# Unpadded value rows, and due times and port flags for the dense layer's first f64 splits

## The chip, the cores and the metric

The kernel runs on one core of one Trainium2 chip. The metric is the time of one execution on the device in microseconds; of several executions the median is taken. A profiled execution is one more run, with the hardware profiler on.

## What is computed

Three layers follow each other on 3072 tokens of 384 numbers (4 batches of 768 positions; 8 heads of 48):

```python
state = alpha[:, :, t, :, None] * state + einsum('bhd,bhe->bhde', k[:, :, t], v[:, :, t])
y[:, :, t] = einsum('bhd,bhde->bhe', q[:, :, t], state)          # for each position t

noisy = x @ w_gate + log1p(exp(x @ w_noise)) * noise             # 8 experts, the best two of each token
out[mask] += top2_w[mask, k, None] * (maximum(x[mask] @ w1[e], 0) @ w2[e])   # w1 384 x 1024

h = x @ w_in                                                     # 384 x 2048, float64 weights
return (maximum(0.01 * h, h) @ w_out).astype(float32)
```

The first is attention with a decaying state, the second a mixture of experts, the third a dense layer. Its two weight matrices are float64, all other inputs are float32.

## The kernel before

**Stages.** Attention takes 24 chunks of 128 positions (`build_unit(u)`). A chunk has three loads on SP's queue: decays `at` (L1058), keys and queries `kq` (L1062), values `nv` (L1066), with 5, 4 and 5 buffers. VectorE scans the decays (L1083, L1090) and scales keys and queries (L1104, L1110); TensorE makes the scores (L1145), the state's update (L1180, with 48 columns of a head's values) and the chunk's output (L1205, with 64 columns of a head's values as the stationary block, so that the two heads of a pair fill partitions 0 to 63 and 64 to 127). Values come padded from 48 to 64 columns for each head, so the columns above 48 are zero. The output is turned by a matmul with `turn_w` (L1235), whose rows 48 to 63 and 112 to 127 are zero, so what stands in those rows of the output has no effect. Every four chunks the tokens are routed: VectorE ranks the experts, and GpSimd scatters the rows (L1341) to `x_s`.

The experts then run as 16 groups of rows (two for each of 8 experts; expert 7's are groups 14 and 15), and the dense layer as 7 groups of tokens (16 to 22). A group has 8 steps (experts) or 16 steps (dense) of a first product (L808, nine matmuls into `ph`), an activation on ScalarE and VectorE (`hh`, `hl`), and a second product (L856, into `py`), which follows two steps later (LAG = 2). Each float32 factor is split into a high and a low part, and three products are added. A group of the dense layer first fetches the two expert results of each of its tokens by row (L888, GpSimd), weighs and adds them (`combine`, L895 on ScalarE and L897 on VectorE), and turns them (L622).

**Weights.** A pair is the weights of two steps. Expert weights are fetched and split into high and low parts by ScalarE (L523) and by VectorE or GpSimd (L527). The dense layer's float64 weights are the pairs E * NP to E * NP + 7 (`last_weights`): each is fetched in five parts, and each part goes through a chain of seven steps (`f64_split`): ScalarE scales (L344, L345), VectorE shifts (L349), joins (L352) and masks (L356), ScalarE rounds (L360), VectorE subtracts (L364), GpSimd multiplies and adds (L367, L368). Both results are stored in `w_d` (L552) and loaded again when a slot for weights is free (L557). Buffers for two chains exist (F64B = 2).

**The order of the work.** Nothing is scheduled by hand: while the program is built, a planner takes all steps (`Planner.add`), each with an engine, a duration, what it waits for, and a due time, and simulates the engines. `prepare` works due times back from a step's users (minus their durations, 0.8 us where the engine changes) and through the buffer rings; after that it takes the lower of this and the step's `own`. `run` picks for an engine the step that can start first, and among those the one that is due first; that order becomes the order of the engine's queue. A step with `port=True` on VectorE or GpSimd also starts, in the plan, no earlier than the last such step on either of the two ended. Loads with a `size` (in MB) pass one after another through a planned DMA of 0.25 MB/us. The plan adds no wait on the chip; the chip waits for data and buffers alone. A step that ran with `port` before: masks, decay and carry of attention, the low parts of expert weights (L527), routing's last part.

## Time and profile before

| | us |
|---|---|
| median of 3 runs | 1014.15 (1011.5 to 1016.0) |
| profiled execution | 1017.89 |
| its span, first to last instruction | 1016.2 |
| TensorE busy | 991.9 |
| VectorE busy | 554.9 |
| ScalarE busy | 378.1 |
| GpSimd busy | 253.8 |

Attention fills about the first 145 us of the span, the experts run to about 599 us and the dense layer to the end. A busy TensorE is not one at its peak: its matmuls overlap, so a matmul's own time says less than the distance from one start to the next. All times of rows below are microseconds from the span's start unless ns stands there. In the names of engines DVE is VectorE, ACT ScalarE, POOL GpSimd, PE TensorE, and SPq the queue of SyncE that issues loads and stores.

### The profile page before, as it was taken

The page shows a single profiled execution, that of the slowest core. Times are in us where ns is not written, and L with a number is a line of the kernel's source. Part 1 is how long each engine was busy: PE and PEld are TensorE (multiplying, and loading weights), DVE is VectorE, ACT ScalarE, POOL GpSimd, SP SyncE. Part 2 cuts the span into 40 slices and gives each one's busy share as a digit, 9 for nine tenths or more (in the row PEclk, how much of TensorE's full clock was granted, in tenths as well). Part 3 has the DMA queues.
Part 4 walks back from the last instruction along what each step waited for, and adds up shares of the span by engine and source line. Part 5 has one row for each costly group of instructions (what it writes and reads, how often), then busy time and mean ns, then how long its engine had stood idle before and what let it go on. Part 6 is the DMA issues. An engine that isn't in the chain of part 4 may idle for free.

```text
span 1016.2 us, 17660 instructions
## 1 busy us (share of the span) xinstructions
PE 991.9 (98%) x6533; PEld 940.4 (93%) x6533; DVE 554.9 (55%) x1208; ACT 378.1 (37%) x796; POOL 253.8 (25%) x311
## 2 busy tenths in 40 slices
PE   8999989999999999999999989999999999999997
PEld 7777879999999999999999989999999999999997
DVE  7998957224635546544644357645545445454543
ACT  5666555224534535454543233312212213121211
POOL 4376874002122314342212235301103002000000
PEclk9999999999999999999999999999999999999999
DMA  9988948423734546555568464301202102010000
GB/s 233 231 254 264 307 151 263 140 90 123 229 124 135 177 152 203 183 169 171 186 211 292 158 196 125 127 1 31 63 1 58 37 1 71 8 40 1 24 1 27
DMA packets 79091, 133.55 MB, mean 131 GB/s; under 512 B 8450, under 2 KB 56708, under 8 KB 78980
## 3 DMA queue, kind: packets, MB, share of 16 engines
q1 hardware_dynamic: 72852, 113.46, 36.4%
q0 software_dynamic: 6144, 18.88, 5.6%
q8 instruction: 53, 0.87, 0.4%
q14 instruction: 42, 0.34, 0.1%
HBM read 93.48 MB, written 39.62 MB: 131 GB/s over the span
## 4 chain that ended last, share of the span: by engine, by line
PE 85%; DMA 7%; DVE 4%; ACT 2%; issue 1%; POOL 1%; SPq 0%; ACTq 0%; DVEq 0%; POOLq 0%
PE ph L808 40%; PE py L856 39%; DMA at<-in_al_l_dram 4%; PE py L852 1%; PE pA L622 1%; PE pB L622 1%; DMA kq<-in_kq_l_dram 1%; DVE pT L1090 1%; PE pS L1145 1%; PE pY L1205 1%; DMA x_s<-xg,si 1%; DMA w2s<-in_moe_w_dram 1%; PE pA L1235 1%; DVE pF L1083 1%; DMA w1s<-in_moe_w_dram 1%
## 5 line engine op out<-in xcount | busy, mean ns | idle before, releaser
L856 PE MATMUL py<-w2hA,hh 128*128 128x384 f32 x768 | 220.6, 340 | 0.0
L856 PE MATMUL py<-w2hB,hh 128*128 128x384 f32 x768 | 217.2, 337 | 0.0
L836 DVE SCALAR_TENSOR_TENSOR hh<-ph,hh 128x384 fp32r<-128x384 f32 (+4 forms) x176 | 77.0, 460 | 178.9 <-ACT hh L826 178.4
L818 ACT ACTIVATE hc<-ph 128x384 f32<-128x384 f32 (+1 forms) x112 | 60.1, 537 | 295.2 <-PE ph L808 295.2
L821 DVE SCALAR_TENSOR_TENSOR hc<-hc 128x384 f32<-128x384 f32 (+1 forms) x112 | 69.5, 620 | 172.4 <-ACT hc L818 172.3
L826 ACT ACTIVATE hh<-ph 128x384 fp32r<-128x384 f32 (+4 forms) x128 | 65.0, 508 | 220.9 <-PE ph L808 184.0
L856 PEld LDWEIGHTS py<-w2hA,hh 128*128 128x128 f32 x768 | 141.0, 188 | 1.5
L856 PEld LDWEIGHTS py<-w2hB,hh 128*128 128x128 f32 x768 | 140.8, 188 | 1.5
L856 PE MATMUL py<-w2lA,hh 128*128 128x384 f32 x384 | 129.4, 337 | 0.0
L808 PE MATMUL ph<-xh,w1hB 128*128 128x384 f32 (+3 forms) x360 | 128.3, 356 | 0.8 <-ACT xh L626 0.6
L856 PE MATMUL py<-w2lB,hh 128*128 128x384 f32 x384 | 128.8, 335 | 0.0
L808 PE MATMUL ph<-xh,w1hA 128*128 128x384 f32 (+4 forms) x360 | 127.9, 355 | 0.1
L808 PE MATMUL ph<-xl,w1hB 128*128 128x384 f32 (+3 forms) x360 | 127.6, 354 | 0.0
L808 PE MATMUL ph<-xh,w1lB 128*128 128x384 f32 (+3 forms) x360 | 127.4, 354 | 0.0
L808 PE MATMUL ph<-xh,w1lA 128*128 128x384 f32 (+4 forms) x360 | 127.3, 353 | 0.0
L808 PE MATMUL ph<-xl,w1hA 128*128 128x384 f32 (+4 forms) x360 | 126.8, 352 | 0.0
L888 POOL DMA_INDIRECT xg<-y_d,gidx x48 | 49.7, 1036 | 255.7 <-PE pB L622 165.9
L856 PEld LDWEIGHTS py<-w2lA,hh 128*128 128x128 f32 x384 | 72.1, 188 | 1.4
L856 PEld LDWEIGHTS py<-w2lB,hh 128*128 128x128 f32 x384 | 72.1, 188 | 1.3
L808 PEld LDWEIGHTS ph<-xh,w1hB 128*128 128x128 f32 x360 | 68.1, 189 | 4.2 <-ACT xh L626 0.8
L808 PEld LDWEIGHTS ph<-xh,w1lA 128*128 128x128 f32 x360 | 67.6, 188 | 4.4
L808 PEld LDWEIGHTS ph<-xh,w1lB 128*128 128x128 f32 x360 | 68.0, 189 | 3.8
(187 smaller groups left out, 1513.0 us busy)
## 6 DMA issues: line engine op xcount, KB each, us to landing
w1s<-in_moe_w_dram SPq DMA_DIRECT2D x32, 384.0 KB, 4.2
w2s<-in_moe_w_dram SPq DMA_DIRECT2D x32, 384.0 KB, 4.4
kq<-in_kq_l_dram SPq DMA_DIRECT2D x24, 448.0 KB, 6.4
xg<-x_s SPq DMA_DIRECT2D x48, 192.0 KB, 2.5
y_d<-ys SPq DMA_DIRECT2D x48, 192.0 KB, 2.2
nv<-in_v_l_dram SPq DMA_DIRECT2D x24, 256.0 KB, 8.5
w1s<-in_moe_w_in_dram SPq DMA_DIRECT2D x24, 256.0 KB, 3.5
w2s<-in_moe_w_out_dram SPq DMA_DIRECT2D x16, 384.0 KB, 3.4
```

Of the source, the lines that this page charges most:

```text
L622: pe.last = nc.tensor.transpose(p[:, d, :n], src[:n, d * 128:(d + 1) * 128], identf[:n, :n])
L808: pe.last = nc.tensor.matmul(ps[:, :n], a[:, d, fo:fo + 128], x[:, d, :n], start=i == 0, stop=i == len(seq) - 1)
L818: nc.scalar.activation(hc[:, :n], ps[:, :n], AF.Copy)
L821: nc.vector.scalar_tensor_tensor(hc[:, :n], hc[:, :n], 0.01, hc[:, :n], op0=OP.mult, op1=OP.max)
L826: nc.scalar.activation(hh[:, :n], ps[:, :n], AF.Relu)
L836: nc.vector.scalar_tensor_tensor(dst, ps[:, a:b], 0.0, hh[:, a:b].bitcast(FT), op0=OP.max, op1=OP.subtract)
L852: pe.last = nc.tensor.matmul(py[:2 * n, :], HT[si, "both"][:, o:o + 2 * n], w[:, f % 2, :], start=(f == 0 and i == 0), stop=(f == nf - 1 a ...
L856: pe.last = nc.tensor.matmul(py[:n, :], h[:, o:o + n], w[:, f % 2, :], start=(f == 0 and i == 0), stop=(f == nf - 1 and i == 2))
L888: return nc.gpsimd.indirect_dma_start(out=yg, out_offset=None, in_=y_d[0:rows, :], in_offset=bass.IndirectOffsetOnAxis(ap=gidx[:, c, kk:kk ...
L1083: nc.vector.tensor_tensor_scan(rev(suf_f[:, 0:NW - 1]), rev(d["at"][:, 1:NW]), rev(heads_f[:, 1:NW]), 1.0, OP.mult, OP.add)
L1090: nc.vector.tensor_tensor_scan(wt, d["at"][:, i * half:(i + 1) * half], heads_f[:, i * half:(i + 1) * half], 0.0, OP.mult, OP.add)
L1145: pe.last = nc.tensor.matmul(d["pa", i][:, p], d["kt"][r, p], d["qp"][r, p], start=True, stop=True)
```

## The change

Values are stored for the kernel as rows of 8 x 48 numbers and 16 zeros (400 columns) in place of 8 x 64 (512). The buffer, the load's planned size (0.26 to 0.2 MB) and the two matmuls' slices follow. The stationary block of L1205 still has 64 columns; its last 16 are now the next head's first values.

In `last_weights` the seven steps of each chain of the first two dense pairs get an `own` due time, and in all eight pairs the steps 2, 5 and 6 of a chain (L352, L364, and L367 with L368) get `port`. The combine's second step (L897) gets `port` too.

```diff
@@ -769,10 +769,11 @@
                 k = 1.0 if m % 2 == 0 else 1.27
                 durs = (0.88, 0.43, 0.92, 0.58, 0.44, 0.46, 1.72)
                 chain = []
+                own = tm[0] + 15 + 10 * (i - E * NP) if i < E * NP + 2 else 1e9
                 for n, eng in enumerate("avvvavg"):
                     use = [(chain[0], r) for r in (R["f64"], R["f64o"])] if n else [(fe, R[nm])]
                     chain.append(add(eng, durs[n] * k, lambda m=m, n=n: split64(i, m, n), chain[-1:], use=use,
-                                     takes=[] if n else [R["f64"], R["f64o"]], phase=2))
+                                     takes=[] if n else [R["f64"], R["f64o"]], phase=2, own=own, port=n in (2, 5, 6)))
                 for which, st in enumerate((chain[4], chain[6])):
                     parts.append(add("s", 0.07, lambda m=m, which=which: spill64(i, m, which), [st],
                                      use=[(chain[0], R["f64o"])], size=0.13 * k, phase=2))
@@ -917,7 +918,7 @@
                     ga, gb = (add("g", 1.29, lambda j=j, kk=kk: gather2(key[2], j, kk), deps, takes=[R["xg"]], lat=3.0,
                                   phase=2, rows=2) for kk in range(2))
                     ca = add("a", 0.5, lambda j=j: combine(key[2], j, 0), use=[(ga, R["xg"])], phase=2)
-                    cb = add("v", 0.64, lambda j=j: combine(key[2], j, 1), [ca], use=[(ga, R["xg"]), (gb, R["xg"])], phase=2)
+                    cb = add("v", 0.64, lambda j=j: combine(key[2], j, 1), [ca], use=[(ga, R["xg"]), (gb, R["xg"])], phase=2, port=True)
                     GX[key + (j,)] = ga
                     AUX[key, j] = [cb]
                     ga.holders[R["xg"]].append(cb)
@@ -1062,12 +1063,12 @@
                 nc.sync.dma_start(d["kq"].rearrange("p a h c -> p (a h c)"), kq_l[u])
 
             def load_v():
-                d["v"] = loads.tile([128, H, 64], FT, name="nv", bufs=5)
-                nc.sync.dma_start(d["v"].rearrange("p h d -> p (h d)"), v_l[u * C:(u + 1) * C, :])
+                d["v"] = loads.tile([128, Dm + 64 - D], FT, name="nv", bufs=5)
+                nc.sync.dma_start(d["v"], v_l[u * C:(u + 1) * C, :])
 
             LA = d["LA"] = add("s", 0.46, load_al, takes=[R["at"]], size=0.23)
             LK = d["LK"] = add("s", 0.46, load_kq, takes=[R["kq"]], size=0.46)
-            LV = d["LV"] = add("s", 0.46, load_v, takes=[R["nv"]], size=0.26)
+            LV = d["LV"] = add("s", 0.46, load_v, takes=[R["nv"]], size=0.2)
 
             def check():
 
@@ -1177,7 +1178,7 @@
                     for p in range(HP):
                         for i in range(2):
                             r = slice(64 * i, min(64 * i + 64, PP))
-                            pe.last = nc.tensor.matmul(d["pu"][r, p, :], d["kN"][:, p, r], d["v"][:, 2 * p + i, 0:D],
+                            pe.last = nc.tensor.matmul(d["pu"][r, p, :], d["kN"][:, p, r], d["v"][:, (2 * p + i) * D:(2 * p + i + 1) * D],
                                              start=p == 0, stop=True, skip_group_check=True)
 
                 def step():
@@ -1202,7 +1203,7 @@
                     room_y()
                 for p in range(HP):
                     for i in range(2):
-                        pe.last = nc.tensor.matmul(d["py"][64 * i:64 * i + 64, p], d["v"][:, 2 * p + i, :], d["am"][:, i, p, :],
+                        pe.last = nc.tensor.matmul(d["py"][64 * i:64 * i + 64, p], d["v"][:, (2 * p + i) * D:(2 * p + i) * D + 64], d["am"][:, i, p, :],
                                          start=p == 0, stop=first, skip_group_check=True)
 
             def across():
@@ -1602,7 +1603,7 @@
     return {
         "al_l": al,
         "kq_l": _np.ascontiguousarray(kq.reshape(kq.shape[0], 64 + d, -1)),
-        "v_l": _np.pad(inputs["v"].transpose(0, 2, 1, 3), ((0, 0), (0, 0), (0, 0), (0, 64 - d))).reshape(b * s, h * 64),
+        "v_l": _np.pad(inputs["v"].transpose(0, 2, 1, 3).reshape(b * s, h * d), ((0, 0), (0, 64 - d))),
         "wgn_l": _np.ascontiguousarray(wgn.reshape(-1, 128, 2 * e).transpose(1, 0, 2)),
         "wgp_l": _np.ascontiguousarray(wgp.reshape(h // 2, 128, -1).transpose(1, 0, 2)),
         "noise_l": _np.ascontiguousarray(inputs["moe_noise"].reshape(n // 128, 128, e).transpose(1, 0, 2)),
```

## Rows read from the trace of the kernel before

**Rows 1.** The page: the span, and each engine's busy time (share) xinstructions.

```profile
span 1016.2 us, 17660 instructions
PE 991.9 (98%) x6533; PEld 940.4 (93%) x6533; DVE 554.9 (55%) x1208; ACT 378.1 (37%) x796; POOL 253.8 (25%) x311
```

**Rows 2.** Busy time by stages; after the engines: granted clock, DMA share, GB/s.

```profile
40.00:60.00 20.00, 18.67 (x256) 15.84 (x257) 18.30 (x53) 14.28 (x36) 10.08 (x15) 1.00 0.99 239
60.00:80.00 20.00, 18.45 (x270) 16.28 (x268) 18.96 (x55) 11.81 (x28) 14.45 (x20) 1.00 0.82 255
...
400.00:500.00 100.00, 100.00 (x576) 98.06 (x575) 55.47 (x120) 48.92 (x103) 31.68 (x29) 1.00 0.57 180
```

**Rows 3.** Chain that ended last, loads in attention: start us, us, what.

```profile
3.62 9.38 DMA kq<-in_kq_l_dram
13.02 8.51 DMA at<-in_al_l_dram
...
22.04 9.32 DMA at<-in_al_l_dram
...
45.10 9.02 DMA at<-in_al_l_dram
...
74.88 5.81 DMA at<-in_al_l_dram
```

**Rows 4.** DMA, 0 to 60 us: packets; issues xcount, KB each, us to landing.

```profile
DMA packets 6068, 14.13 MB, mean 235 GB/s; under 512 B 878, under 2 KB 1008, under 8 KB 6059
...
kq<-in_kq_l_dram SPq DMA_DIRECT2D x15, 448.0 KB, 7.2
at<-in_al_l_dram SPq DMA_DIRECT2D x16, 226.2 KB, 9.1
nv<-in_v_l_dram SPq DMA_DIRECT2D x13, 256.0 KB, 9.0
```

**Rows 5.** Lines on VectorE: xcount: ns min/median/max, first and last start us, forms.

```profile
L352 DVE SCALAR_TENSOR_TENSOR f64f<-f64e,f64f x40: 402/428/1196, 275.6 to 617.8; 128x256 uint32<-128x256 uint32 x24, 128x384 uint32<-128x384 uint32 x16
...
L356 DVE TENSOR_SCALAR f64e<-f64f x40: 281/294/1885, 278.1 to 621.2; 128x256 uint32<-128x256 uint32 x24, 128x384 uint32<-128x384 uint32 x16
...
L364 DVE TENSOR_TENSOR f64f<-f64f,f64h x40: 409/542/1842, 281.4 to 628.6; 128x256 f32<-128x256 f32 x24, 128x384 f32<-128x384 f32 x16
...
L897 DVE SCALAR_TENSOR_TENSOR xg<-xg,wts x24: 606/614/1432, 588.2 to 899.6; 128x384 f32<-128x384 f32 x24
```

**Rows 6.** Timeline of VectorE and GpSimd before the dense layer: start us, us, what.

```profile
595.23 1.43 DVE L897 SCALAR_TENSOR_TENSOR xg<-xg,wts 128x384 f32<-128x384 f32 x1
...
595.25 1.00 POOL L368 TENSOR_TENSOR f64g<-f64f,f64g 128x384 fp32r<-128x384 f32 x1 [0.91 <-DVE f64f L364]
```

**Rows 7.** Timeline of TensorE there; in brackets its idle time and what ended it.

```profile
596.81 0.52 PE L622 MATMUL pB<-identf,xg 128*128 128x128 f32 x3 [1.08 <-DVE xg L897]
598.21 0.52 PE L622 MATMUL pA<-identf,xg 128*128 128x128 f32 x3 [0.88 <-DVE xg L897]
599.31 0.69 PE L808 MATMUL ph<-xh,w1hB 128*128 128x384 f32 x1 [0.58 <-ACT xh L626]
...
602.63 0.39 PE L808 MATMUL ph<-xh,w1hB 128*128 128x384 f32 x1
...
604.27 0.34 PE L808 MATMUL ph<-xh,w1hB 128*128 128x384 f32 x1
```

**Rows 8.** The stage behind it, columns as in rows 2.

```profile
599.30:606.00 6.70, 6.69 (x28) 6.39 (x29) 2.97 (x7) 0.98 (x2) 0.00 (x0) 0.75 0.60 221
```

**Rows 9.** Timelines: pair 7's last w1 reload (SP), its first matmul (TensorE).

```profile
631.95 0.32 SPq L557 DMA_DIRECT2D w1lA<-w_d  x1
...
646.50 0.34 PE L808 MATMUL ph<-xh,w1hA 128*128 128x384 f32 x1
```

**Rows 10.** DMA, whole span: w1's low part, xcount, KB each, us to landing.

```profile
w1lA<-w_d SPq DMA_DIRECT2D x4, 384.0 KB, 5.1
```

## Prediction

> **What bounds the kernel now.** I read the page first. The span is 1016.2 us and TensorE is busy for 991.9 us of it [rows 1], so at most 24.3 us of TensorE idle time can be won at all, plus what matmuls lose to waiting in a queue that counts as busy. Next I read the table by stages [rows 2]: from 400 to 500 us TensorE is busy 100.00 of 100.00 us, with VectorE at 55.47 and GpSimd at 31.68. In that stretch nothing that happens on VectorE or GpSimd reaches the end of the kernel, and the f64 splits run there (the first start near 275 us, the last near 618 us [rows 5]). From 40 to 80 us, in the attention stage, no engine is full, but TensorE has 18.5 to 18.7 us of 20 and VectorE 18.3 to 19.0, and the DMA engines are at 0.99 and then 0.82 of their time [rows 2].
>
> Which of them ends last there is read from the chain of work [rows 3]. Before 60 us four of its pieces are loads: `kq` for 9.38 us and `at` for 8.51, 9.32 and 9.02 us, 36.2 us together. After that the longest such piece is 5.81 us. A load of 226 KB takes 9 us to land because others are ahead of it: in the first 60 us 14.13 MB move at 235 GB/s, and 44 loads are issued [rows 4]. So in that stretch bytes cost time, though the engines are nearly full behind them.
>
> The second place where the chain can still be shortened is the start of the dense layer. There TensorE stands idle 1.08, 0.88 and 0.58 us, twice for the combine of L897 and once for ScalarE [rows 7], and after that the granted clock of the stretch is 0.75 [rows 8]: the nine matmuls of a first product take 3.32 us from 599.31 to 602.63, the next nine 1.64 us [rows 7]. The lower of the two levels, 1.2 GHz, costs 3.32 - 1.64 = 1.7 us. Idle and clock make 2.54 + 1.7 = 4.2 us.
>
> **Part 1, values without padding.** A `nv` load falls from 256 KB [rows 4] to 128 rows of 400 floats, 200 KB: 56 KB less of the 226.2 + 448 + 256 = 930 KB that a chunk loads, 6.0%. Removed: 57344 bytes at 235 GB/s, 0.244 us of all DMA engines for each load. No instruction is added or taken away; the matmuls of L1180 and L1205 keep 48 and 64 columns. Columns 48 to 63 of a stationary block now hold the next head's first values; they land in rows that `turn_w` multiplies by zero.
>
> If the stage were paced by loads to its last chunk, 24 x 0.244 = 5.9 us would go. If engines pace it, nothing goes. I take the share of the chain: 6.0% of the 36.2 us of load waits gives 2.2 us, and 6.0% of the later 5.81 us gives 0.3, together 2.5 us. The row nearest to this is the 0.99 of DMA time from 40 to 60 us, which speaks for the upper half; the 18.3 us of VectorE beside it speaks for the lower. The smaller size (0.26 to 0.2) also enters the planner's clock for loads, so that SP's order, and with it all queues of this stage, may come out otherwise. A load that moves one place back waits for one more: 448 KB at 235 GB/s, 1.95 us. The bounds are thus -5.9 and +2.0.
>
> The Trainium skill (DMA: Bandwidth & Descriptors, section "How a descriptor splits into AXI transactions") speaks against full credit: a transfer that doesn't begin on a multiple of 256 bytes also fetches the bytes before it. Rows of 2048 bytes all begin on one; of rows of 1600 bytes one in four does. An estimate from that page is 96 bytes more for a mean row, so 17% saved of each load in place of 22%, and 1.9 us in place of 2.5. No row shows it here: `at`, with rows of 2068 bytes, lands in 9.1 us beside 9.0 for `nv` [rows 4], but both times are mostly queue.
>
> **Part 2, `own`.** It costs and gives nothing, by arithmetic on the planner. A due time is already worked back from the users, and `own` can only lower it. It is 15 us (25 us for the second pair) after the start of expert 7's first group in the planner's clock. A chain's durations sum to 5.43 us (6.90 for a `w_out` part); with 0.8 us for each of four changes of engine and 0.87 for the spill it is 9.5 to 11. With two buffers (F64B = 2) chain k waits for chain k - 2, so the first of 40 chains lies 19 links, some 195 us, ahead of the last, and the tenth 15 links, some 155 us. The last must be done before pair 7's product: two groups of some 25 us and 14 steps of 3.2 us, so 96 us after that group's start. The first two pairs are then due between about 110 and 70 us before the group starts. The minimum of that and +15 or +25 is unchanged. Price: 0 us.
>
> **Part 3, `port`.** Three of a chain's seven steps (the second VectorE step, the subtraction, the GpSimd pair) and the combine of L897 now wait, in the plan only, until the planner's port is free. No wait is added on the chip; the order in VectorE's and GpSimd's queues changes, then ScalarE's and SP's (spills, reloads). Up to 550 us TensorE hides all that. At the dense start it doesn't: the combine before the first transposes took 1.43 us while GpSimd ran a split of 1.00 us that began 0.02 us later [rows 6], against a median of 0.61 us [rows 5]. That is 0.82 us too much with TensorE waiting behind it. Keeping them apart gives at most the 4.2 us above. It can also cost: a combine planned behind a GpSimd pair of about 2 x 1.00 us comes 2.0 us later. I take the combine's own 0.8 us, since it is the one excess with TensorE right behind it.
>
> The Trainium skill (SBUF - State Buffer, section "Who interferes with whom") says that single-source operations in a 2-port mode take the shared pair too, and that the second to start blocks fully. The trace agrees: L356, a single-source operation left without the flag, takes 294 ns in the median and 1885 at most [rows 5]. By that rule the change protects only two of a chain's four VectorE steps; the price, 1.6 us for a hit, falls where TensorE hides it.
>
> **The sum.** 2.5 + 0 + 0.8 = 3.3 us less. The profiled execution took 1017.89 us, 1.7 of it outside the span; so 1014.6 us for one like it. The median of the runs is 1014.15, 3.7 under the profiled one; against it 1010.9 us. The parts are in series (the dense layer can't start before attention has ended), so they add.
>
> **Rivals.**
> *Loads pace the whole stage, and the dense start heals.* Then 5.9 us go in the first stage, and 0.8 to 4.2 us at 592 to 603: 1007.5 to 1004.1. For it: four load waits in 60 us, and a stage in which every engine waits in turn. Against it: VectorE at 18.96 us of 20 from 60 to 80 us [rows 2], when DMA time has fallen to 0.82.
>
> *It does nothing.* The loads are prefetched, VectorE and TensorE pace the stage, and the order at the dense start comes out much the same: 1014. For it: 92 to 95% busy engines.
>
> *The last dense weights come late (the slower side).* The place is pair 7. Its last `w1` part is issued at 631.95 us [rows 9] and lands some 5.1 us later [rows 10], at 637.0; its first matmul starts at 646.50 [rows 9]. The margin is 9.5 us. A flagged VectorE step finds GpSimd busy with chance 0.32 (31.68 of 100 us [rows 2]) and waits half a pair, 1.0 us: 0.64 us for the two of a chain. Chains follow each other through two buffers, so over 20 links that is 12.8 us. Faster subtractions (542 ns in the median, 409 alone [rows 5]) and the like give back some 0.26 us a chain, 5.2 in all. Net 7.6 us, inside the margin. Without the refund it is 3.3 us past it, with waits twice as long 16. The point from which it decides is 9.5 us; at a typical 8 us the time is 1014.15 - 2.5 + 8 = 1019.7. Against it: as dues draw near, the planner puts these steps first.
>
> **How the numbers follow.** A measurement of this kernel can tell about 0.5%, 5 us, from no change. The forecast (part of the load waits go: 1009.1 to 1013) has a chance of 0.47, the full gain 0.30, nothing 0.11, late weights 0.12. Faster by over 0.5% (under 1009.1) is the full gain, 0.30; slower by over 0.5% (above 1019.2) is the late weights, 0.12; within it is the rest, 0.58. The range is 1004 to 1018.5: below it the full gain, above it nothing, the +2.0 us ends of parts 1 and 3 and the smaller late weights.
>
> **What would show it.** Right: `nv` at 200 KB, 1.3 MB fewer bytes in all; `at` landing under 9.1 us in the first 60 us; the last L1205 group some 2.5 us earlier; no change of order from `own` alone; L897 nowhere near 1.43 us at the dense start, and TensorE idle under 2.54 us there. Wrong: `at` waits as long as before (then engines paced the stage), a wait of TensorE on L557's reloads near 646 us (late weights), or new waits of TensorE between 200 and 550 us (then the new order on VectorE holds up `hh` and `hl`, which I priced at nothing). The prediction fails most easily through the new order in the first stage, which the trace before can't show.

## The result, and the profile after

| kernel | median of runs, us | lowest to highest | profiled execution / its span |
|---|---|---|---|
| before, the three runs ahead of the prediction | 1014.15 | 1011.5 to 1016.0 | 1017.89 / 1016.2 |
| before, twelve runs beside the changed kernel | 1011.25 | 1009.82 to 1016.0 | - |
| changed | 1018.24 | 1015.88 to 1022.26 | 1017.89 / 1016.2 |

The change makes the kernel slower: ratio 1.0067, interval 1.0048 to 1.0085, so 5 to 9 us. The forecast was 1010.9, 0.3% faster.

The two profiled spans are equal, and a reader who compares only them would see no change. The profiled execution of before was a long one: 1017.89 us where twelve runs lie between 1009.82 and 1016.0. Part 2 of the change alone leaves every queue as it was (below, e1_own), so its trace is a second execution of the same queues: span 1011.2. It stands for before from here on.

The changed kernel's span and bytes, and its stage from 40 to 60 us (columns as in [rows 2]):

```profile
span 1016.2 us, 17647 instructions
...
DMA packets 79091, 132.18 MB, mean 130 GB/s; under 512 B 8450, under 2 KB 59780, under 8 KB 78980
...
40.00:60.00 20.00, 18.62 (x272) 16.12 (x271) 19.05 (x57) 13.82 (x35) 11.93 (x18) 1.00 0.68 211
```

DMA time from 40 to 60 us fell from 0.99 [rows 2] (0.94 in e1_own) to 0.68. VectorE rose from 18.30 to 19.05 of 20 us, but not because the loads are out of the way: e4_port below, with padded values and a DMA time of 0.95, has 19.23. The loads land sooner (DMA from 0 to 60 us, as in [rows 4]; then the two loads left in the chain of that stretch, as in [rows 3]):

```profile
kq<-in_kq_l_dram SPq DMA_DIRECT2D x15, 448.0 KB, 6.2
at<-in_al_l_dram SPq DMA_DIRECT2D x16, 226.2 KB, 6.3
nv<-in_v_l_dram SPq DMA_DIRECT2D x15, 200.0 KB, 7.2
```

```profile
16.34 6.78 DMA at<-in_al_l_dram
23.18 6.46 DMA nv<-in_v_l_dram
```

`at` lands in 6.3 us, not 9.1 [rows 4], and the chain of the first 60 us has 13.2 us of loads where it had 36.2 [rows 3]. But e1_own, with padded values, has 6.8 us for `at` and 11.7 us of loads there:

```profile
0.82 2.85 DMA at<-in_al_l_dram
41.98 8.80 DMA at<-in_al_l_dram
```

Where the time went is told by when stages begin. The table gives, in us from the start of the span, the first matmul of L808 (L809 in the changed kernel: from line 773 on its lines stand one further down) of a group, worked out from TensorE's timeline; the half-clock stretch at the end, which all have, is left out. Groups 0 to 15 are the experts', 16 and later the dense layer's.

| execution | group 0 | group 2 | 16 | 17 | 18 | end | stretch at half clock |
|---|---|---|---|---|---|---|---|
| before (e1_own) | 141.3 | 188.0 | 594.1 | 644.6 | 711.8 | 1011.2 | 594.4 |
| changed | 139.5 | 188.6 | 593.5 | 647.7 | 716.7 | 1016.2 | 594.5, 649.1 |
| e2_vbytes | 140.3 | 187.0 | 593.1 | 643.7 | 710.9 | 1010.3 | 78.8, 594.2 |
| e3_v | 140.6 | 190.3 | 597.3 | 646.6 | 713.8 | 1013.5 | 12.4, 142.1 |
| e4_port | 141.6 | 190.1 | 595.4 | 648.2 | 718.1 | 1017.9 | 107.5, 646.8 |
| e5_port_hold | 139.8 | 186.5 | 591.9 | 640.9 | 708.1 | 1007.6 | none |
| e15_v_dve | 139.8 | 187.8 | 594.8 | 645.5 | 712.8 | 1012.3 | 11.8, 595.5 |
| e11_both | 140.9 | 188.2 | 593.9 | 642.8 | 710.1 | 1009.7 | 64.4 |

Between the first two rows the attention is 1.8 us shorter (executions of one order differ by more: the first profile of before has group 0 at 146.1), groups 0 and 1 are 2.4 us longer, groups 2 to 15 1.2 us shorter, and dense groups 16 and 17 5.5 us longer (123.2 against 117.7). Two places lose.

The place that was forecast to gain does gain. TensorE at the dense start (as [rows 7]; brackets: idle time and what ended it), then L898, the combine's VectorE half, over the span (as [rows 5]):

```profile
590.13 0.52 PE L622 MATMUL pB<-identf,xg 128*128 128x128 f32 x3 [0.28 <-DVE xg L898]
592.44 0.52 PE L622 MATMUL pA<-identf,xg 128*128 128x128 f32 x3 [0.74 <-DVE xg L898]
593.54 0.45 PE L809 MATMUL ph<-xh,w1hB 128*128 128x384 f32 x1 [0.58 <-ACT xh L626]
```

```profile
L898 DVE SCALAR_TENSOR_TENSOR xg<-xg,wts x24: 599/612/1129, 580.0 to 899.4; 128x384 f32<-128x384 f32 x24
```

Idle time is 1.60 us where it was 2.54. Fifty us later the same flags lose more. The last instructions of ScalarE in group 16, the matmul of TensorE that waited for them, and the stage (columns as [rows 2]; granted clock near the end):

```profile
641.86 0.62 ACT L896 ACTIVATE xg<-xg,wts 128x384 f32<-128x384 f32 x1 [4.88 <-DMA xg<-y_d,gidx]
644.21 0.61 ACT L896 ACTIVATE xg<-xg,wts 128x384 f32<-128x384 f32 x1 [1.74 <-DMA xg<-y_d,gidx]
645.73 0.61 ACT L896 ACTIVATE xg<-xg,wts 128x384 f32<-128x384 f32 x1 [0.90 <-DMA xg<-y_d,gidx]
646.69 0.61 ACT L896 ACTIVATE xg<-xg,wts 128x384 f32<-128x384 f32 x1 [0.35 <-DMA xg<-y_d,gidx]
647.22 0.85 ACT L819 ACTIVATE hc<-ph 128x384 f32<-128x384 f32 x2
```

```profile
647.74 0.50 PE L809 MATMUL ph<-xh,w1hB 128*128 128x512 f32 x1 [3.11 <-ACT hc L819]
```

```profile
646.00:656.00 10.00, 8.26 (x33) 7.30 (x34) 4.84 (x10) 2.91 (x6) 0.00 (x0) 0.83 0.01 3
```

Four combines for the rows of a later group stand ahead of the last two `hc` copies of this one (an `hc` copy, L818 or L819, takes a first product out of `ph`). They wait for gathers, the last of which GpSimd issues at 643.53; a gather lands some 3.2 us later (median), and the fourth combine runs at 646.69. The `hc` copies, whose input TensorE had finished, wait behind them, and TensorE waits 3.11 us. Then the clock is granted at half for 3.41 us. GpSimd issues the last gather no later than in e1_own (643.85 there); what changed is the order on ScalarE. In the execution of before the same two copies run between the combines and wait only for TensorE:

```profile
638.27 0.62 ACT L895 ACTIVATE xg<-xg,wts 128x384 f32<-128x384 f32 x1 [0.78 <-DMA xg<-y_d,gidx]
641.37 0.62 ACT L895 ACTIVATE xg<-xg,wts 128x384 f32<-128x384 f32 x1 [2.47 <-DMA xg<-y_d,gidx]
643.19 0.49 ACT L818 ACTIVATE hc<-ph 128x384 f32<-128x384 f32 x1 [1.21 <-PE ph L808]
644.75 0.49 ACT L818 ACTIVATE hc<-ph 128x384 f32<-128x384 f32 x1 [1.07 <-PE ph L808]
645.65 0.62 ACT L895 ACTIVATE xg<-xg,wts 128x384 f32<-128x384 f32 x1 [0.41 <-DMA xg<-y_d,gidx]
```

### The profile page after: what moved, and what is told of

It reads as the page before. It is cut to its first block, busy times and chain, and to the rows that moved or that the text cites. A ratio compares the mean times of both kernels' runs of the same rounds, so it can differ in the third digit from the quotient of the medians.

```text
span 1016.2 us, 17647 instructions
## 1 busy us (share of the span) xinstructions
PE 991.2 (98%) x6529; PEld 940.0 (93%) x6529; DVE 559.3 (55%) x1205; ACT 381.1 (37%) x799; POOL 254.8 (25%) x311
## 2 busy tenths in 40 slices
DMA packets 79091, 132.18 MB, mean 130 GB/s; under 512 B 8450, under 2 KB 59780, under 8 KB 78980
## 3 DMA queue, kind: packets, MB, share of 16 engines
q1 hardware_dynamic: 72852, 112.08, 34.8%
## 4 chain that ended last, share of the span: by engine, by line
PE 84%; DVE 5%; DMA 4%; issue 2%; ACT 2%; POOL 1%; SPq 0%; POOLq 0%; ACTq 0%; DVEq 0%
PE ph L809 39%; PE py L857 38%; PE py L853 1%; PE pA L622 1%; DMA w2s<-in_moe_w_dram 1%; DVE pF L1084 1%; PE pB L622 1%; DVE pT L1091 1%; DMA xg<-y_d,gidx 1%; DMA at<-in_al_l_dram 1%; PE pA L1236 1%; PE pS L1146 1%; DMA nv<-in_v_l_dram 1%; PE pM L1037 1%; DMA x_s<-xg,si 1%
## 5 line engine op out<-in xcount | busy, mean ns | idle before, releaser
L819 ACT ACTIVATE hc<-ph 128x384 f32<-128x384 f32 (+1 forms) x112 | 60.1, 538 | 292.4 <-PE ph L809 291.9
L809 PE MATMUL ph<-xh,w1hB 128*128 128x384 f32 (+3 forms) x360 | 128.5, 357 | 3.7 <-ACT hc L819 3.1
L809 PE MATMUL ph<-xh,w1hA 128*128 128x384 f32 (+4 forms) x360 | 127.9, 355 | 0.7 <-DVE hh L837 0.7
L809 PE MATMUL ph<-xh,w1lA 128*128 128x384 f32 (+4 forms) x360 | 127.4, 354 | 0.9 <-POOL w1lA L527 0.8
L809 PE MATMUL ph<-xh,w1lB 128*128 128x384 f32 (+3 forms) x360 | 128.0, 355 | 0.0
L809 PE MATMUL ph<-xl,w1hB 128*128 128x384 f32 (+3 forms) x360 | 127.8, 355 | 0.1
L809 PE MATMUL ph<-xl,w1hA 128*128 128x384 f32 (+4 forms) x360 | 126.8, 352 | 0.0
L809 PEld LDWEIGHTS ph<-xh,w1hB 128*128 128x128 f32 x360 | 68.2, 189 | 7.0 <-ACT hc L819 3.4
L809 PEld LDWEIGHTS ph<-xh,w1lA 128*128 128x128 f32 x360 | 67.6, 188 | 5.9 <-POOL w1lA L527 1.0
L840 DVE TENSOR_TENSOR hh<-hc,hh 128x384 fp32r<-128x384 f32 (+1 forms) x112 | 70.0, 625 | 3.6
```

What stands on the lines that cost most here:

```text
L809: pe.last = nc.tensor.matmul(ps[:, :n], a[:, d, fo:fo + 128], x[:, d, :n], start=i == 0, stop=i == len(seq) - 1)
L819: nc.scalar.activation(hc[:, :n], ps[:, :n], AF.Copy)
L840: nc.vector.tensor_sub(hl[:, :n], HT[si, "hc"][:, :n], hh[:, :n].bitcast(FT))
```

## The experiments

Ratios are to runs of before on the same chip, with a 95% interval.

**The four parts by themselves.**

e1_own takes the due times alone:

```diff
- takes=[] if n else [R["f64"], R["f64o"]], phase=2))
+ takes=[] if n else [R["f64"], R["f64o"]], phase=2, own=tm[0] + 15 + 10 * (i - E * NP) if i < E * NP + 2 else 1e9))
```

> The due times for the first two pairs alone. Working the due times by hand says that they change nothing, so that every engine's queue keeps its order: ratio 1.000, within the spread of the kernel before (about 1010 to 1016 us). It is thus also a second profile of the order before: if the first stage of the first profile (first products at 146.1 us) was only an unlucky execution, this one starts them several us earlier (139 to 142). Rival: the due times do move steps; then the time moves by several us and queues differ.

1.0011 (0.9998 to 1.0025), every queue as before. Part 2 is nothing, as worked out.

e2_vbytes takes the values without padding, but leaves the planned size of their load at 0.26:

```diff
- d["v"] = loads.tile([128, H, 64], FT, name="nv", bufs=5)
+ d["v"] = loads.tile([128, Dm + 64 - D], FT, name="nv", bufs=5)
  LV = d["LV"] = add("s", 0.46, load_v, takes=[R["nv"]], size=0.26)
```

> Unpadded values, but the planned size of the load left at 0.26 MB, so that the order on the computing engines is that of before and only 56 KB less are loaded per chunk. Theory that loads pace the first stage: 1 to 3 us less (ratio 0.997 to 0.999). Rival, engines pace it: 1.000. Theory that the unpadded load itself is the loss: ratio about 1.005 with longer landing times of nv.

0.9993 (0.9979 to 1.0006), with the queues of the four engines as before. The bytes alone are worth 0.7 us; the interval reaches from 2.1 us gained to 0.6 us lost. DMA time from 40 to 60 us is 0.73 in it (0.94 in e1_own), and group 0 starts at 140.3, 1.0 us sooner.

e3_v takes the planned size with it:

```diff
- LV = d["LV"] = add("s", 0.46, load_v, takes=[R["nv"]], size=0.26)
+ LV = d["LV"] = add("s", 0.46, load_v, takes=[R["nv"]], size=0.2)
```

> Unpadded values with the planned size of 0.2 MB: the order changes in attention and the first expert groups, not after them. Theory that the port flags are the loss: ratio 0.995 to 1.000. Rival, the new order of the first stage is the loss: ratio about 1.007, with first products later than in the kernel before.

1.0049 (1.0029 to 1.0069). One number that only the planner reads costs about 5 us. Its order differs from e2_vbytes in the attention and the first groups only.

e4_port takes the flags alone:

```diff
- takes=[] if n else [R["f64"], R["f64o"]], phase=2))
+ takes=[] if n else [R["f64"], R["f64o"]], phase=2, port=n in (2, 5, 6)))
- cb = add("v", 0.64, ..., phase=2)
+ cb = add("v", 0.64, ..., phase=2, port=True)
```

> The port flags alone (f64 chains and combine), values padded as before. Theory that the flags are the loss: TensorE waits some 3 us for ScalarE's hc near 645 us, as in the changed kernel, and the granted clock falls after it; ratio 1.005 to 1.009. Rival, the values' new order is the loss: ratio 1.000, and no such wait.

1.0044 (1.0028 to 1.0060). It has the same wait as the changed kernel and a longer stretch at half clock, 6.83 us. The waits of TensorE from 636 to 652 us (us in total, times, longest), and the stage:

```profile
PE ph L808 <- ACT hc L818: 3.6, 1, 3.6
```

```profile
646.00:656.00 10.00, 7.83 (x25) 6.70 (x26) 4.97 (x10) 2.58 (x5) 0.00 (x0) 0.66 0.03 12
```

So there are two losses of some 5 us, one in each part of the change that does anything. Added they make 9.4 us, where the change lost 6.8 (4.9 to 8.6); the intervals meet.

**The flags: is it ScalarE's queue?** e5_port_hold holds back the gathers, and with them the combines that stood in the way:

```diff
- deps = ready_at[c] + out_rows[0] + (...)
+ deps = ready_at[c] + out_rows[0] + (...) + ([S1[steps.index((2 * E + 1, 0, nf))]["g1"]] if gi > 2 * E + 1 else [])
```

> The port flags alone, as in e4_port, and one added dependency: the gathers of dense group 18 (the third) and later may not be planned before the first product of group 17. That leaves TensorE's and SyncE's queues of e4_port as they are; on ScalarE it takes the six combines L895 of group 18's rows out from between the hc copies of group 16, so that none stands ahead of its last two hc. Theory (ScalarE's queue): e4_port loses its time because those combines wait for gathers which GpSimd issues late, and hc behind them makes TensorE wait 3.64 us near 648 us, after which the granted clock is at half for 6.83 us. Then here that wait is gone, dense group 16 lasts 50.3 to 50.8 us again (52.8 in e4_port), group 17 some 67.2 to 67.9 (69.9), and the time falls from 1016.6 to 1011.3 to 1012.3 us, ratio 1.000 to 1.001. Rival (late chains): the f64 splits themselves, with TensorE's and SyncE's queues as in e4_port, make the weights of a late pair late; then the wait at 648 us only changes its name (to a reload L557 or a spill) and the time stays 1015.5 to 1017.5. Rival (moved on): the combines of group 18 now come too late or delay the hc of group 17, and 1 to 3 us come back between 650 and 720 us: 1012.5 to 1014.5.

0.9980 (0.9969 to 0.9990): not only is the loss gone, the flags now gain 1 to 3 us. TensorE's and SyncE's queues are those of e4_port. The `hc` copies of group 16 (ScalarE) wait only for TensorE, and TensorE has no wait from 636 to 720 us:

```profile
639.50 0.49 ACT L818 ACTIVATE hc<-ph 128x384 f32<-128x384 f32 x1 [5.70 <-PE ph L808]
641.06 0.49 ACT L818 ACTIVATE hc<-ph 128x384 f32<-128x384 f32 x1 [1.07 <-PE ph L808]
```

```profile
646.00:656.00 10.00, 10.00 (x53) 9.14 (x52) 6.33 (x12) 3.92 (x7) 4.19 (x4) 1.00 0.49 148
```

Groups 16 and 17 last 116.2 us (122.7 in e4_port). On GpSimd the last two pairs of split steps now stand ahead of gathers, so the last chain ends 9.1 us ahead of pair 7's first product (6.7 in e4_port); the trace of e4_port gives its wait to `hc` alone and shows none for a reload, which speaks against the rival of late chains, though e5 by itself doesn't separate the two.

e7_hold is its control, the added dependency in the kernel before, without the flags.

> The kernel before with nothing but the added dependency of e5_port_hold (gathers of group 18 and later not planned before the first product of group 17). TensorE's, GpSimd's and SyncE's queues are those of before; ScalarE and VectorE take group 18's combines later. A control: it prices the dependency by itself. If the combines have slack of a whole group (67 us), 1011.0 to 1011.9, ratio 0.9995 to 1.0005. If the two or three combines that the kernel before has among the last hc of group 16 cost something there, it is 0.3 to 1.0 us faster. If they get in the way of group 17's hc, 0.5 to 2 us slower.

1.0010 (0.9993 to 1.0026). The dependency by itself gains nothing; what e5 gains is the flags'.

e10_after_hold adds that dependency to the changed kernel.

> The changed kernel with the added dependency of e5_port_hold alone (gathers of group 18 and later not planned before the first product of group 17); nothing of its first 560 us is touched, so the order that comes with the smaller planned size stays. If the two losses add (dependency worth 5 to 7 us in e5_port_hold against e4_port, 0.998 against 1.0044), the time falls from 1018.2 to 1011.5 to 1013.5 us, ratio 1.000 to 1.003: e3_v's 4.9 us, less the 2.0 us that the flags gained once repaired. If the dependency repairs only what e4_port had and not this kernel, 1016 to 1018.5.

1.0021 (1.0007 to 1.0035), where the change had 1.0067. The dependency repairs the changed kernel too, and what stays is the first loss, lessened by the flags' gain.

**The planned size: is it GpSimd's queue?** At the end of the attention GpSimd splits the first expert's weights (L527) between scatters of routed rows (L1341). GpSimd's timeline after the last masks and decay (done at 134.7 and 135.0 us) in e2_vbytes, then in e3_v:

```profile
134.84 1.01 POOL L1341 DMA_INDIRECT x_s<-xg,si  x1 [0.17 <-issue]
136.16 0.97 POOL L1341 DMA_INDIRECT x_s<-xg,si  x1 [0.30 <-issue]
137.14 1.84 POOL L527 TENSOR_TENSOR w1lA<-w1s,w1hA 128x768 fp32r<-128x768 f32 x1
139.14 1.00 POOL L1341 DMA_INDIRECT x_s<-xg,si  x1 [0.16 <-issue]
140.15 1.87 POOL L527 TENSOR_TENSOR w2lA<-w2s,w2hA 128x768 fp32r<-128x768 f32 x1
```

```profile
135.18 1.01 POOL L1341 DMA_INDIRECT x_s<-xg,si  x1 [0.17 <-issue]
136.49 0.98 POOL L1341 DMA_INDIRECT x_s<-xg,si  x1 [0.30 <-issue]
137.78 0.98 POOL L1341 DMA_INDIRECT x_s<-xg,si  x1 [0.30 <-issue]
139.06 0.97 POOL L1341 DMA_INDIRECT x_s<-xg,si  x1 [0.30 <-issue]
140.03 1.84 POOL L527 TENSOR_TENSOR w1lA<-w1s,w1hA 128x768 fp32r<-128x768 f32 x1
142.04 1.00 POOL L1341 DMA_INDIRECT x_s<-xg,si  x1 [0.17 <-issue]
143.06 1.84 POOL L527 TENSOR_TENSOR w2lA<-w2s,w2hA 128x768 fp32r<-128x768 f32 x1
```

With the new order GpSimd has two scatters more left when these are done, and both splits come 2.9 us later. TensorE waits for the first one, in e3_v and in the changed kernel alike:

```profile
141.93 0.50 PE L808 MATMUL ph<-xh,w1lA 128*128 128x320 f32 x1 [0.80 <-POOL w1lA L527]
```

```profile
140.84 0.41 PE L809 MATMUL ph<-xh,w1lA 128*128 128x320 f32 x1 [0.79 <-POOL w1lA L527]
```

The next weight fetch waits too, since the split frees its buffer: two fetches of L514 hold SyncE's queue from 130.33 to 139.4 us in e2_vbytes, from 129.84 to 142.3 in e3_v. Groups 0 and 1 last 49.7 us there against 46.7, and 49.1 in the changed kernel.

e6_v_first gives the two splits a due time of their own: `own=131.0 if i == 0 and on == "g" else 1e9` at L761 of e3_v.

> The unpadded values with the smaller planned size, as in e3_v, and a due time of 131 us of their own for the two GpSimd weight splits L527 (w1lA and w2lA) of the first expert's first pair. On GpSimd this moves w1lA from behind four scatters L1341 to behind one, and nothing else on that engine before it. Theory (GpSimd's queue at the end of the attention): e3_v loses 4.9 us because w1lA comes 2.9 us later (140.03 against 137.14 us in e2_vbytes), TensorE waits for it, and the weight staging buffer that it frees holds back the next weight fetches. Then w1lA starts before 138 us here, group 0 lasts 20.5 to 21.5 us (25.3 in e3_v, 20.7 in e2_vbytes), and the time is 1011.0 to 1012.5, ratio 1.000 to 1.001. Rival (scatters): the three scatters now come later, and the first rows L589 or L724 wait for them; group 0 starts or ends 2 to 4 us late all the same: 1014 to 1017. Rival (the attention's order): the loss lies in the new order of the attention itself; then nothing changes: 1016 to 1017.

1.0111 (1.0096 to 1.0126), slower still, though w1lA starts at 135.64. The due time also moved the next pairs' weight copies on ScalarE and splits on VectorE ahead of the first products' follow-ups, which then wait behind them for weights: TensorE waits once for 8.4 us, for `hh` (L836). The experiment does not isolate what it was meant to. e8_after_fix, the changed kernel with this and e5's dependency, shares the fault.

> The changed kernel with both repairs, the due time of e6_v_first and the dependency of e5_port_hold. Theory: the whole of the 6.8 us lies in the two queues, so both repairs together give back nearly all of it: 1010.5 to 1012.5, ratio 0.999 to 1.001; the bytes saved and the planned port by themselves are then worth at most 1 us. If only one of the two holds, 1013.5 to 1015; if neither, 1018. Rival (the forecast gain appears): with the queues repaired, the unpadded loads and the combine without GpSimd beside it give the 3.3 us that were forecast: 1007.5 to 1009.

1.0087 (1.0071 to 1.0102), with an 8.5 us wait at the same place. It says nothing on the rest.

e9_v_defer keeps the plan of e3_v and changes only when three scatters are issued on GpSimd: behind w1lA.

```diff
- ins = st.fn(e) if len(st.eng) > 1 else st.fn()
+ (scatters 32 to 34 are kept, and issued right after the next split_lo on GpSimd)
```

> Plan and queues of e3_v to the instruction on TensorE, ScalarE, VectorE and SyncE; on GpSimd alone the three scatters L1341 that stood right ahead of w1lA (L527) are issued right behind it. This is what e6_v_first could not do, where a due time also moved the weight copies on ScalarE and VectorE and the weight fetches. Theory (GpSimd's queue): w1lA starts near 136 us (140.03 in e3_v, 137.14 in e2_vbytes), TensorE's 0.80 us wait for it at 141.9 us goes, and the weight fetches behind its staging buffer, so the 0.5 us wait near 170 us too, with the half-clock stretch of 3.41 us at 142.1 us; groups 0 and 1 together last 46.5 to 47.3 us (49.7 in e3_v, 46.7 in e2_vbytes) and the time is 1012.0 to 1013.5 us, ratio 1.000 to 1.002. Rival (other queues): the loss lies in ScalarE's, VectorE's or SyncE's new order after the attention, which stays; then the two groups last 49 us or more and the time is 1015.5 to 1017. Rival (scatters): the later scatters hold back rows, and a wait for L589 or L724 rows takes the place: 1014 to 1017.

1.0026 (1.0014 to 1.0039): about half of the loss is back, though the intervals of the two ratios overlap. w1lA starts 4.4 us ahead of group 0's first product and is not waited for. But w2lA, now behind four scatters, comes at 145.31 and runs beside L252, a step of the routing on VectorE that takes 0.23 us in e3_v and 1.78 us here. An `hh` stands behind it in VectorE's queue, and TensorE waits for that. VectorE, GpSimd, TensorE:

```profile
145.46 1.78 DVE L252 TENSOR_TENSOR g_um<-g_um,g_ru 128x32 f32<-128x32 f32 x1
```

```profile
145.31 1.87 POOL L527 TENSOR_TENSOR w2lA<-w2s,w2hA 128x768 fp32r<-128x768 f32 x1
```

```profile
150.35 0.38 PE L808 MATMUL ph<-xh,w1hA 128*128 128x320 f32 x1 [1.63 <-DVE hh L836]
```

e12_v_defer2 does the same with scatters 30 to 33, behind both splits.

> Again the queues of e3_v to the instruction on TensorE, ScalarE, VectorE and SyncE; on GpSimd four scatters L1341 are issued later, behind both weight splits L527 of the first pair: one that stood ahead of the last masks L1154 of the attention, and the three right ahead of w1lA. From the last masks on GpSimd's queue is then: masks, one scatter, w1lA, one scatter, w2lA (e2_vbytes: masks, two scatters, w1lA, one scatter, w2lA; e9_v_defer put three more scatters ahead of w2lA). Theory (all of it is GpSimd's queue; e9 got back half since it moved w2lA back by three scatters): w2lA starts within 3.5 us of w1lA, no wait of TensorE over 0.5 us for w1lA or hh between 140 and 175 us, groups 0 and 1 together 46.5 to 47.5 us, ratio 0.998 to 1.001. Rival (half lies in the other queues): ratio 1.002 to 1.004 as in e9, with the waits for hh near 150 or 170 us still there. Rival (late scatters): TensorE or SyncE waits for rows; 1.003 or more.

1.0053 (1.0033 to 1.0073): nothing is back. TensorE waits for neither split, and now the scatters are late. The chain waits for one from 143.64 for 4.38 us, the next fetch of scattered rows (L589) is issued at 148.99 (145.60 in e3_v), and TensorE waits for `sel`, a step of the next routing, ahead of which VectorE stands idle for 4.67 us:

```profile
157.06 0.17 PE L656 MATMUL pA<-acc,ones_b 128*128 128x8 bf16 x1 [3.26 <-DVE sel L1322]
```

Each of the two orders on GpSimd brought a wait of its own. That points at the amount left, not at its order, and e15_v_dve takes work off: the plan of e3_v, the two splits issued on VectorE.

```diff
- lambda en=on[0], m=m: split_lo(i, m, en), [hi],
+ lambda en=on[0], m=m: split_lo(i, m, "v" if i == 0 else en), [hi],
```

> The plan of e3_v, but the two weight splits L527 of the first expert's first pair (w1lA and w2lA) are issued on VectorE instead of GpSimd, at the place that the plan gives them; TensorE's, ScalarE's and SyncE's queues stay, GpSimd's loses just these two (1.84 us each) and keeps its scatters in order. e9 and e12 changed the order within GpSimd's queue, and each got a new wait there. Theory (GpSimd's backlog: with the new order it has some 2.9 us more to do when the attention ends, whichever comes last): with 3.7 us taken off it the loss is gone: groups 0 and 1 together 46.3 to 47.5 us, no wait over 0.7 us between 140 and 175 us, ratio 0.998 to 1.001. Rival (the other engines' order): ratio 1.003 to 1.006 as e3_v. Rival (VectorE instead): the splits of about 0.95 us each hold up the gate's steps or hh there, and a wait for VectorE takes the place: 1.001 to 1.004.

1.0016 (1.0000 to 1.0031), against 1.0049 for e3_v. e16_vb_dve prices the same move in the order of before:

> The same move of the two splits to VectorE in the order of before (unpadded values, planned size 0.26, as e2_vbytes at 0.9993). A control: it prices the move itself. Theory: there GpSimd's backlog kept nothing waiting (no wait of TensorE over 0.2 us between 140 and 195 us), so 0.998 to 1.001. If the move by itself gains over 0.2%, e15's gain is not the repair of an order.

0.9988 (0.9975 to 1.0000), against 0.9993 for e2_vbytes. The order costs 0.0056 with the splits on GpSimd (1.0049 less 0.9993) and 0.0028 with them on VectorE (1.0016 less 0.9988). The difference, half of the loss, is what GpSimd's backlog would cost, but it is known only to some 0.003 either way, so these four ratios alone don't show that it is more than nothing. The traces show the piece that goes: TensorE's wait for w1lA (0.80 us in e3_v) is gone in e15_v_dve. What stays, in the profiled executions: groups 0 and 1 hold 1.3 us (48.0 against 46.7, with waits of 0.19 and 0.46 us for `hh` near 167 us), and group 15 1.0 us. It lasts 31.9 us in e3_v and 31.8 in e15_v_dve, 30.9 in e1_own and e2_vbytes, and a combine in it waits 3.2 us for its gather in place of 1.9. That second piece is not tied to the order: the queues there are the same in all four, and e16_vb_dve, with the order of before, has 31.4. Where the rest of the loss comes from stays open.

e13_vb23 and e14_vb21 are unpadded values with planned sizes of 0.23 and 0.21, each with an order of its own.

> Unpadded values with a planned size of 0.23 (between 0.26 of before and 0.2 of the change): a third order of the attention, in which GpSimd has one scatter ahead of the last masks and four between them and w1lA, as e3_v has four there. Theory (GpSimd's queue): as late a w1lA as in e3_v and the same loss in groups 0 and 1, 2 to 3 us, ratio 1.002 to 1.006. Rival (it is the special order of e3_v on the other engines): 0.998 to 1.001.

> Unpadded values with a planned size of 0.21: a fourth order, three scatters between the last masks and w1lA, two ahead of the masks. Theory (GpSimd's queue): w1lA one scatter (1.3 us) earlier than with four, one later than with two: between e2_vbytes and e3_v, ratio 1.000 to 1.004. Rival (special order of e3_v): 0.998 to 1.001. If it falls outside both, the place of w1lA doesn't order these runs.

1.0009 (0.9992 to 1.0026) and 1.0013 (0.9999 to 1.0027). w1lA starts at 137.44 and 137.59 us, as early as in e2_vbytes, although e13 has four scatters ahead of it: GpSimd did them sooner. Counting scatters, as the expectation for e13 did, was the wrong measure; when GpSimd is through fits these two runs. They also show that not every new order costs 5 us.

**A version with what helped.** e11_both has the unpadded values with the old planned size, the flags, and e5's dependency.

> A version meant to be faster than both kernels: unpadded values with the old planned size (the order of before in the first stage, e2_vbytes, 0.9993), the port flags and the dependency of e5_port_hold (0.998). If the two add, 0.9973 with some 0.0015 either way: 1007 to 1010 us. Rival (the bytes are worth nothing, as e2_vbytes says): the same as e5_port_hold, 0.9975 to 0.9985. Rival (they collide): 0.999 to 1.001.

0.9955 (0.9939 to 0.9971), 1010.06 against 1013.53 us on the same chip: faster than both kernels, by about what the change was forecast to bring. The two parts multiplied give 0.9973; the intervals meet. Its queues are those of e5_port_hold, so the two differ by the bytes alone: 0.0025 (0.0006 to 0.0044), 0.6 to 4.4 us. With e2_vbytes (at most 2.1 us) that leaves some 1 to 2 us for the bytes.

## Why the prediction was wrong

*What bounds the kernel.* TensorE first, with splits hidden from 400 to 550 us: held, and no new wait of TensorE shows between 200 and 550 us. But the four loads in the chain of the first 60 us were taken for the stage's, and they are some executions' only. Of the five profiled executions with padded values and this order of the attention, before and e7_hold have such a chain (36.2 us in [rows 3] and 34.8; group 0 at 146.1 and 145.0), and e1_own, e4_port and e5_port_hold have not (11.7, 2.8 and 10.0 us; 139.8 to 141.6). In a stage whose engines are 92 to 95% busy a chain names the last of several near ties. Of the three without padding in the same order (e2_vbytes, e11_both, e16_vb_dve) none has it; three are too few to show that the bytes spare it.

*Part 1, -2.5 us: the term failed twice.* Its size: loads did land sooner, by more than the 6.0% (6.3 for 9.1 us, 6.8 in e1_own), and gave 0.7 us, near the "nothing" bound (e2_vbytes). Its other bound: the +2.0 us for the new order was priced as one load moved one place back in SyncE's queue. The order cost some 5 us (e3_v), and TensorE's new waits there are not for loads but for w1lA, which GpSimd splits 2.9 us later, and for `hh` behind it. GpSimd had more left to do at the end of the attention, where the first groups need both its scatters and its splits; by e15_v_dve that is about half of the loss, with a wide error, and the other half stays open. The prediction named "the new order in the first stage" as where it fails most easily, and still gave it no case of its own.

*Part 2, 0 us:* right, queue for queue.

*Part 3, -0.8 us: the gain came, the loss was not seen.* In all twelve profiled executions without the flags the last but one combine ahead of the dense layer takes 1.43 to 1.45 us; in all six with them it takes 0.61. VectorE's timeline in e3_v and e5_port_hold:

```profile
593.24 1.44 DVE L897 SCALAR_TENSOR_TENSOR xg<-xg,wts 128x384 f32<-128x384 f32 x1
```

```profile
587.78 0.61 DVE L897 SCALAR_TENSOR_TENSOR xg<-xg,wts 128x384 f32<-128x384 f32 x1
```

So the excess of 0.82 us went as forecast. TensorE's idle time there fell by less, from 2.2 to 2.6 us without the flags to 1.6 to 2.3 with them, but a stretch at half clock follows the dense start in ten of the twelve executions and in two of the six. Once repaired, the flags gain 2.0 us (e5_port_hold). The step that failed is the sentence that the order changes in VectorE's and GpSimd's queues, "then ScalarE's and SP's (spills, reloads)", with no cost for ScalarE: that order cost 4.5 us (e4_port), through one wait of TensorE for `hc`. In the queues as they are built, the combine's flag alone changes nothing, and the flags on the split steps alone put the four combines ahead of the two `hc` copies (neither was run alone): in the plan the gathers are there in time, and on the chip they are not yet. The bounds of +2.0 at most looked at the dense start alone, not at the end of its first group.

The Trainium skill (SBUF - State Buffer, section "Who interferes with whom") was cited for two of a chain's VectorE steps being left without protection. The traces agree for L349, single-source and without the flag: of its 24 instructions on 128x256, 4 run beside arithmetic of GpSimd in e2_vbytes and 10 in e5_port_hold, and those take 0.42 and 0.80 us in the mean, the others 0.29. But L352, with the flag, got no shorter either; groups of VectorE to 720 us (busy, mean ns of one; idle before), e2_vbytes, then e5_port_hold:

```profile
L352 DVE SCALAR_TENSOR_TENSOR f64f<-f64e,f64f 128x256 uint32<-128x256 uint32 x24 | 12.7, 529 | 0.4
...
L349 DVE TENSOR_SCALAR f64f<-f64e 128x256 uint32<-128x256 uint32 x24 | 7.3, 308 | 2.6 <-ACT f64e L344 2.6
```

```profile
L352 DVE SCALAR_TENSOR_TENSOR f64f<-f64e,f64f 128x256 uint32<-128x256 uint32 x24 | 14.4, 599 | 0.3
L349 DVE TENSOR_SCALAR f64f<-f64e 128x256 uint32<-128x256 uint32 x24 | 12.0, 502 | 5.0 <-ACT f64e L344 5.0
```

So the flags did not keep the splits apart on the chip: more of them met, where TensorE hides it, and the one meeting that it waited for went.

*The rival of late weights* came to its edge, with its sum nearly right and its price wrong. Pair 7's last `w1` part (SyncE) and first matmul (TensorE) in the changed kernel, as [rows 9]:

```profile
635.97 0.32 SPq L557 DMA_DIRECT2D w1lA<-w_d  x1
...
640.90 0.34 PE L809 MATMUL ph<-xh,w1hA 128*128 128x384 f32 x1
```

From the issue to the matmul 14.55 us were left before, 4.93 now: chains came 9.6 us later against the products, where 7.6 were worked out and 9.5 allowed. So the margin was just used up. The third matmul of the pair, the first that reads `w1lA`, starts 0.48 us after the second in place of 0.18, since its weight load (PEld) waits for the reload:

```profile
641.56 0.19 PEld L809 LDWEIGHTS ph<-xh,w1lA 128*128 128x128 f32 x1 [0.46 <-DMA w1lA<-w_d]
```

That is 0.3 us of the loss; the case was priced at a typical 8 us. In e4_port, with the same 4.93 us, nothing waits there.

*The sum against the median* was the smaller error: 1014.15 was a median of three, 2.9 us over that of the twelve. The forecast ratio, 0.997, doesn't depend on it. That 1018.24 lies inside the stated range (1004 to 1018.5) is luck: the upper end was made of late weights, of two ends of +2.0 us and of that median, not of the two losses.

*The signs.* Nearly all signs of being right came: `nv` at 200 KB, 132.18 MB moved where 133.55 were, `at` at 6.3 us, the last L1205 at 134.3 us (136.1 in e1_own), no queue moved by `own`, the combine at 0.61 us and 1.60 us of idle time. None of them looked where the losses lie.

## What to carry over

In a kernel whose order comes from a planner, a number that only the planner reads is a change to every queue: cost it by asking, at the end of each stage, what each in-order engine still has ahead of the work that the next stage needs. A step that waits for a transfer costs an in-order engine everything behind it, so place it behind the work that feeds the busiest engine. And before a gain is read from one chain of waits in a stage with no clear bound, compare it with a second execution of the same program.

## What was not expected of the hardware

Idle time of TensorE was followed by a stretch at the lower clock in some executions and not in others. After the 3.11 us from 644.6 in the changed kernel the granted clock is at half for 3.41 us, and with the 3.64 us of e4_port for 6.83, from 646.8 on, 1.4 us before that wait ends. At the dense start idle pieces of 2.58 us in all were followed by 3.41 us at half in e1_own, of 1.60 us in the changed kernel too, and of 2.21 us in e3_v (3.53 with one 7.5 us earlier) by none. Half clock for 3.41 us costs 1.7 us: group 17 lasts 69.0 us in the changed kernel and 67.2 in e1_own. So by an estimate from these rows the two waits cost 4.8 and 6.3 us, 1.5 to 1.7 times their length, and one such stretch is a third of either loss measured here.

A short step on VectorE can last as long as the operation of GpSimd beside it: L252 on 128x32 numbers took 1.78 us beside a split of 1.87 us (e9_v_defer), L236 on as many 2.01 us beside the same split in e10_after_hold, where both take about 0.2 us otherwise. For an order this means that GpSimd's late work can reach TensorE through VectorE, with no wait of TensorE for GpSimd to be seen.
